# A gated delta rule and a cosine feed-forward block on one core: another order of all work, and pair 1's inverses stored by whole partitions

## The chip, the core and the metric

The kernel runs on one core of a Trainium2 chip. Its five engines take their instructions in the order in which the program lists them, each from its own queue: TensorE (PE, matmuls; PEld is its loading of weights), VectorE (DVE), ScalarE (ACT), GpSimd (POOL) and SyncE (SP). In this program SP does nothing but issue DMAs, and ACT issues some DMAs between its own instructions. An instruction that has to wait holds everything behind it on its engine. The metric is the device time of one execution in microseconds (us), as the median over several runs.

## The reference

Two blocks follow each other. The first is a delta rule over 768 tokens for 4 batches and 8 heads of 48 features. The second multiplies its output, 3072 tokens by 384, by a matrix of 384 by 2048, gates with the cosine, and multiplies by 2048 by 384.

```python
B, H, S, D = q.shape                      # 4, 8, 768, 48
k_n = k / (np.linalg.norm(k, axis=-1, keepdims=True) + 1e-06)
state = np.zeros((B, H, D, D), dtype=np.float32)
for t in range(S):
    kt, vt, bt = (k_n[:, :, t], v[:, :, t], beta[:, :, t, None])
    y[:, :, t] = np.einsum('bhd,bhde->bhe', q[:, :, t], state)
    v_old = np.einsum('bhde,bhd->bhe', state, kt)
    state = state + bt[:, :, :, None] * np.einsum('bhd,bhe->bhde', kt, vt - v_old)
x = y.transpose(0, 2, 1, 3).reshape(B * S, H * D)
h = x @ w_in
g = h * np.cos(h)
out = g @ w_out
```

q, k, v and beta are float32. The two weight matrices arrive as 64-bit floats.

## The kernel before

**The delta rule** is cut into 24 units n of 32 tokens (C). A unit holds all 4 batches and 8 heads. Two units make a pair m. The steps of a unit, with the names that the order uses:

- loads of k, q and v: four DMAs each in the first pairs (`load`, L393 to L411; a load of k for a unit from 6 on takes eight). From unit 6 on, `blocks` (four DMAs for keys, four for queries, L421) bring what the PE transposes (`turn`, L677) brought before.
- `square`, `sum`, `norms`, `scale`: the norms of the keys, on ACT, DVE, POOL and DVE. `weigh` scales a pair's v on DVE.
- `turn` and `turn_out`, then `gram` (L704, 64 recorded matmuls): the products of keys with keys and with queries; `gram_keys` and `gram_queries` on DVE.
- the inverse of a triangular 32 by 32 matrix for every batch and head. Units 0 and 1 build it by `double`, six levels of matmuls on PE, each with a turn, a copy or an addition on DVE or ACT before the next (L788 to L819). Every later pair is inverted by columns on POOL (`invert`, L898, whose two lines are L908 and L915), and goes through DRAM to change its layout: `gram_put` stores the products (g to g_dr, L859), `gram_get` loads them with one matrix to a partition (g_dr to gb, two DMAs, L872 or L880), `invert` runs over the columns in seven blocks `inv.m.0` to `inv.m.6`, `put` stores the result (z to z_dr, one DMA, L920) and `get` loads it for PE (z_dr to zt, four DMAs a unit, L939). Pair 1 (HALVED) is inverted in halves of 16 by 16, in four blocks; its `get` takes eight DMAs a unit (L931), which land in w_sum's space. There is one buffer for gb and one for z, so a pair's inverse starts after the one before it has ended.
- `state` (L959), `right` (L976), `solve` (p_u), `solve_out`, `part_out`, `update` (L1075), `update_out`: the chain from one state to the next. For units 2 and 3 two more products, `solve_half` (p_w, L989) and `between` (p_v), stand before `solve`.
- `within` (L1092), `within_out` and `within_half` (copies to y, L1105 and L1119), `features` (a transpose, p_z, L1127), `features_out`: a unit's output as columns for the second block.

**The second block** takes a pair p of units (256 tokens) at a time. Pair 0 is computed plainly: 32 steps `hidden` (L1148, six recorded matmuls each), the gate in four steps (`turns` on ACT, `rest` on DVE, `cos` on ACT, `gate` on DVE), and 32 steps `out` (L1345, two recorded matmuls each). Pairs 1 to 11 use sums that save products: `x_sum` (L1237) and `left` (L1419) are sums of the inputs and of the gates, on POOL or DVE; `layer` (L1322, eight recorded matmuls) is one of 20 first products, and two parts `out` (L1403, eight each) make one of seven second products. `collect` adds them up, `store` writes.

**The weights** come in 28 chunks (`weights`, one DMA each, L550), and each is turned into float32 by `split` (ACT, L560 and L564), `shift` (DVE, L568) and `add` (POOL, L572).

**Warming**: `keep_warm` (L501) multiplies a tile of ones on PE (L503, two recorded matmuls each), and emits nothing once the first `out` has been emitted. Five of them open the program (WARM_FIRST), and the order holds WARMS more.

**The order of the work** comes from a search and stands in the file: `Order.run` (L227) goes through LINE, a list of 2290 numbers, each a task; it emits them in that order, which is then the order on every engine and on the two DMA queues. OTHER (L63) names the tasks that go to a second engine: DMAs to ACT's queue instead of SP's (`queue`, L387), and with `either` (L390) x_sum to DVE instead of POOL, left to POOL instead of DVE, and inv.1.x to DVE instead of POOL. The end of the file pins every engine to this order.

Of the kernel before, what the change touches and what calls it, by code (L numbers as in the profile page):

```python
# [10 lines left out]
FP = mybir.dt.float32  # L11
# [5 lines left out]
C = 32  # L17
DP = 64
SPLIT = 2
# [41 lines left out]
class Order:  # L61

    OTHER = {  # L63
        ('double_eye', 0), ('v', 2), ('gram_put', 2), ('within_half', 2), ('inv', 1, 0),
        ('put', 1), ('within_half', 3), ('q', 4), ('gram_put', 4), ('gram_get', 2),
        ('blocks', 8, 0), ('k', 9), ('gram_get', 4), ('get', 9), ('gram_put', 10),
        ('gram_get', 5), ('k', 12), ('gram_put', 12), ('v', 13), ('v', 14), ('v', 15),
        ('blocks', 16, 0), ('put', 8), ('blocks', 18, 0), ('get', 19), ('v', 20),
        ('blocks', 20, 1), ('gram_put', 20), ('v', 21), ('gram_get', 10), ('put', 10),
        ('v', 22), ('v', 23), ('put', 11), ('get', 23), ('store', 0, 0), ('right', 2, 2),  # L70
        ('in_sums', 4), ('x_sum', 1, 'd'), ('x_sum', 1, 'n'), ('x_sum', 1, 'm'),
        ('x_sum', 1, 'e'), ('x_sum', 1, 'k'), ('x_sum', 1, 'g'), ('x_sum', 1, 'i'),
        ('x_sum', 1, 'f'), ('x_sum', 1, 'b0'), ('left', 1, 1, 0), ('x_sum', 2, 'd'),
        ('x_sum', 2, 'n'), ('x_sum', 2, 'm'), ('x_sum', 2, 'e'), ('x_sum', 2, 'k'),
        ('x_sum', 2, 'g'), ('x_sum', 2, 'i'), ('x_sum', 2, 'l'), ('x_sum', 2, 'b0'),
        ('left', 2, 4, 0), ('x_sum', 3, 'd'), ('x_sum', 3, 'l'), ('x_sum', 3, 'f'),
        ('x_sum', 3, 'h'), ('x_sum', 3, 'b0'), ('left', 3, 4, 1), ('store', 3, 0),
        ('store', 3, 1), ('x_sum', 4, 'i'), ('x_sum', 4, 'f'), ('x_sum', 4, 'h'),
        ('left', 4, 4, 0), ('left', 4, 4, 1), ('left', 4, 3, 0), ('left', 4, 3, 1),
        ('x_sum', 5, 'd'), ('x_sum', 5, 'm'), ('x_sum', 5, 'e'), ('x_sum', 5, 'k'),  # L80
        ('x_sum', 5, 'g'), ('x_sum', 5, 'f'), ('x_sum', 5, 'b0'), ('left', 5, 1, 0),
        ('left', 5, 2, 0), ('left', 5, 1, 1), ('left', 5, 2, 1), ('left', 5, 4, 0),
        ('left', 5, 3, 0), ('store', 5, 0), ('x_sum', 6, 'd'), ('x_sum', 6, 'n'),
        ('x_sum', 6, 'm'), ('x_sum', 6, 'k'), ('x_sum', 6, 'i'), ('x_sum', 6, 'f'),
        ('x_sum', 6, 'h'), ('x_sum', 6, 'b0'), ('left', 6, 1, 1), ('left', 6, 2, 1),
        ('store', 6, 0), ('store', 6, 1), ('x_sum', 7, 'n'), ('x_sum', 7, 'e'),
        ('x_sum', 7, 'i'), ('x_sum', 7, 'h'), ('x_sum', 7, 'b0'), ('left', 7, 2, 1),
        ('left', 7, 4, 0), ('left', 7, 4, 1), ('left', 7, 3, 1), ('store', 7, 0),
        ('store', 7, 1), ('x_sum', 8, 'n'), ('x_sum', 8, 'e'), ('x_sum', 8, 'k'),
        ('x_sum', 8, 'g'), ('x_sum', 8, 'f'), ('x_sum', 8, 'h'), ('x_sum', 8, 'b0'),  # L90
        ('left', 8, 2, 0), ('left', 8, 3, 1), ('store', 8, 1), ('x_sum', 9, 'd'),
        ('x_sum', 9, 'm'), ('x_sum', 9, 'i'), ('x_sum', 9, 'f'), ('x_sum', 9, 'h'),
        ('x_sum', 9, 'b0'), ('left', 9, 1, 0), ('left', 9, 2, 1), ('left', 9, 4, 1),
        ('store', 9, 0), ('x_sum', 10, 'd'), ('x_sum', 10, 'k'), ('x_sum', 10, 'l'),
        ('x_sum', 10, 'f'), ('x_sum', 10, 'h'), ('left', 10, 1, 0), ('left', 10, 2, 0),
        ('left', 10, 3, 0), ('left', 10, 3, 1), ('x_sum', 11, 'k'), ('x_sum', 11, 'i'),
        ('x_sum', 11, 'f'), ('x_sum', 11, 'h'), ('x_sum', 11, 'b0'), ('left', 11, 1, 0),
        ('left', 11, 4, 1), ('store', 11, 1), ('store_right', 11), ('weights', 5),
        ('weights', 7), ('weights', 12), ('weights', 13), ('weights', 14), ('weights', 15),
        ('weights', 19)  # L100
    }

    WARM_FIRST, WARMS = 5, 20
    LINE = """
# [143 lines left out]
def kernel(  # L248
# [34 lines left out]
    B, H, S, D = q.shape  # L283
# [8 lines left out]
    ROWS = C // SPLIT  # L292
# [66 lines left out]
    DOUBLED, HALVED, HC = 2, 1, C // 2  # L359
# [27 lines left out]
    def queue(*key):  # L387
        return nc.scalar if key in Order.OTHER else nc.sync
# [1646 lines left out]
```

## Time and profile before

| | us |
|---|---|
| median of three runs | 633.37 |
| lowest and highest of them | 633.14, 634.39 |
| the profiled execution, as the other runs are timed | 635.52 |
| its span in the trace | 633.7 |

The profiled execution lasts 1.82 us longer than its span, for what lies before the first and after the last instruction. Section 1 of the page has each engine's busy time; section 2 cuts the span in 40 slices of 15.84 us and gives tenths of busy time. A row of the timeline has the start, the length, the engine, the line and the tiles; "[2.06 <-ACT krec L655]" is idle time of the engine just before, and who ended it. "SPq" and "ACTq" rows are instructions of the sequencer, here DMAs that it issues. In rows by line, the last numbers are the busy time, the mean length of one in ns, and the idle time before them.

### The profile page before, as it was taken

How to read it: one execution, taken by the hardware profiler on the slowest of the kernel's cores; microseconds unless marked ns; L12 is line 12 of the kernel's file. 1: busy time of each engine (PE TensorE's matmuls, PEld its weight loads, DVE VectorE, ACT ScalarE, POOL GpSimd, SP SyncE). 2: the span in 40 equal slices, each digit the busy share in tenths (PEclk: the TensorE clock that was granted, in tenths of full speed). 3: DMA queues.
4: the chain of work that ended last, by engine and by line, in shares of the span. 5: the costliest groups of instructions: out<-in, count | busy, mean ns of one | idle time of the engine just before them, and what ended most of it. 6: DMA issues, size and time to landing. Idle time of an engine off the chain costs nothing.

```text
span 633.7 us, 24406 instructions
## 1 busy us (share of the span) xinstructions
PE 611.1 (96%) x10296; PEld 565.9 (89%) x10296; DVE 481.1 (76%) x969; ACT 326.8 (52%) x610; POOL 430.6 (68%) x784
## 2 busy tenths in 40 slices
PE   7887899999999999999999999999999999999997
PEld 6666787887889999999999999999999999999997
DVE  6876768899998888789868778778758567576582
ACT  3545675563662733745635655555544544455340
POOL 5465888888988887885988898875864884120110
PEclk9998999999999999999999999999999999999999
DMA  8986657744553455346435344234312102100001
GB/s 189 224 189 161 142 117 163 147 74 69 99 88 66 85 88 94 64 68 108 68 65 90 60 78 74 46 57 83 59 32 52 33 13 40 23 2 26 1 26 26
DMA packets 215893, 50.51 MB, mean 80 GB/s; under 512 B 207512, under 2 KB 210856, under 8 KB 215784
## 3 DMA queue, kind: packets, MB, share of 16 engines
q1 hardware_dynamic: 172784, 36.18, 31.4%
q10 hardware_dynamic: 42792, 12.53, 9.6%
q8 instruction: 81, 1.33, 0.9%
q0 software_dynamic: 208, 0.25, 0.2%
q14 instruction: 28, 0.23, 0.1%
HBM read 38.68 MB, written 10.22 MB: 77 GB/s over the span
## 4 chain that ended last, share of the span: by engine, by line
PE 69%; DMA 13%; POOL 8%; DVE 3%; issue 2%; ACT 2%; SPq 2%; ACTq 1%; POOLq 0%; DVEq 0%
PE p_out L1403 27%; PE p_h L1322 25%; DMA kp<-in_k_dram 3%; POOL part L908 3%; PE p_kq L959 3%; POOL z L915 3%; PE p_s L1075 2%; DMA qp<-in_q_dram 2%; PE p_kq L1092 2%; PE p_g L715 2%; PE p_out L1345 2%; DMA w_sum<-in_moe_w_out_dram 2%; PE p_h L1403 2%; DMA w_out<-in_moe_w_in_dram 2%; PE p_u L1033 1%
## 5 line engine op out<-in xcount | busy, mean ns | idle before, releaser
L908 POOL TENSOR_TENSOR part<-z,gb 128x126 f32<-128x126 f32 (+23 forms) x321 | 139.9, 436 | 50.1 <-DMA gb<-g_dr 20.7
L915 POOL TENSOR_TENSOR z<-z,part 128x126 f32<-128x126 f32 (+23 forms) x321 | 146.9, 458 | 25.2
L1403 PE MATMUL p_out<-w_out,g_ffn 128*128 128x192 f32 x672 | 121.7, 329 | 0.3 <-DVE g_ffn L1419 0.3
L1403 PEld LDWEIGHTS p_out<-w_out,g_ffn 128*128 128x128 f32 x672 | 107.8, 190 | 1.9 <-DVE g_ffn L1419 0.5
L1201 ACT ACTIVATE turns<-turns,halfpi 128x512 f32<-128x512 f32 x96 | 68.1, 719 | 74.4 <-DVE turns L1192 61.8
L1322 PE MATMUL p_h<-x_sum,w_in 128*128 128x128 f32 x704 | 93.7, 279 | 0.0
L1403 PE MATMUL p_out<-w_sum,g_ffn 128*128 128x192 f32 x496 | 88.8, 328 | 0.2
L1322 PEld LDWEIGHTS p_h<-x_sum,w_in 128*128 128x128 f32 x704 | 86.3, 191 | 2.9 <-ACT p_h L1334 0.2
L1403 PEld LDWEIGHTS p_out<-w_sum,g_ffn 128*128 128x128 f32 x496 | 79.6, 190 | 1.3 <-POOL g_ffn L1419 0.3
L1339 DVE TENSOR_TENSOR g_ffn<-g_ffn,p_h 128x512 f32<-128x512 f32 x88 | 59.7, 680 | 26.7 <-PE p_h L1322 26.2
L1185 ACT ACTIVATE turns<-g_ffn,quarter_turn 128x512 int32<-128x512 f32 x77 | 54.7, 719 | 45.8 <-DVE g_ffn L1204 19.1
L1204 DVE TENSOR_TENSOR g_ffn<-turns,g_ffn 128x512 f32<-128x512 f32 x77 | 55.5, 726 | 18.3 <-ACT turns L1201 18.1
L1192 DVE SCALAR_TENSOR_TENSOR turns<-g_ffn,turns 128x512 f32<-128x512 f32 x77 | 56.8, 747 | 10.5 <-ACT turns L1185 10.4
L1322 PE MATMUL p_h<-x_sum,in_sum 128*128 128x128 f32 x440 | 58.7, 278 | 0.7 <-ACT p_h L1334 0.7
L1322 PEld LDWEIGHTS p_h<-x_sum,in_sum 128*128 128x128 f32 x440 | 54.4, 191 | 2.6 <-ACT p_h L1334 1.0
L1105 ACT COPY y<-p_kq 32x384 f32<-32x384 f32 x88 | 41.3, 469 | 12.4 <-DMA vp<-in_v_dram 7.1
L1419 POOL TENSOR_TENSOR g_ffn<-g_ffn,g_ffn 128x512 f32<-128x512 f32 x14 | 17.9, 1278 | 43.7 <-PE p_out L1403 27.2
L1322 PE MATMUL p_h<-x_ffn,w_in 128*128 128x128 f32 x352 | 46.7, 277 | 0.0
L606 POOL TENSOR_TENSOR knrm<-ksum,halves 128x16 f32<-128x16 f32 (+1 forms) x14 | 36.8, 2625 | 12.5 <-DVE ksum L594 12.5
L1334 ACT COPY p_h<-p_h 128x512 f32<-128x512 f32 x44 | 25.3, 575 | 37.9 <-PE p_h L1322 23.6
L1322 PEld LDWEIGHTS p_h<-x_ffn,w_in 128*128 128x128 f32 x352 | 42.8, 192 | 1.0
L1455 DVE SCALAR_TENSOR_TENSOR o<-p_out,o 128x192 f32<-128x192 f32 x74 | 25.0, 351 | 23.0 <-PE p_out L1403 21.0
(174 smaller groups left out, 1056.8 us busy)
## 6 DMA issues: line engine op xcount, KB each, us to landing
w_sum<-in_moe_w_out_dram SPq DMA_DIRECT2D x11, 384.0 KB
vp<-in_v_dram SPq DMA_DIRECT2D x64, 48.0 KB
kp<-in_k_dram SPq DMA_DIRECT2D x128, 24.0 KB
gb<-g_dr SPq DMA_DIRECT2D x12, 256.0 KB
w_out<-in_moe_w_in_dram SPq DMA_DIRECT2D x5, 512.0 KB
g_ffn<-in_moe_w_in_dram SPq DMA_DIRECT2D x5, 512.0 KB
out_dram<-o SPq DMA_DIRECT2D x12, 192.0 KB
qp<-in_q_dram SPq DMA_DIRECT2D x34, 64.0 KB
```

What stands on the lines that cost most here:

```text
L606: nc.gpsimd.tensor_tensor(out=scales[m][2][:, part], in0=sums[m, part.start][:, 0:n], in1=halves[:, 0:n], op=ALU.pow,)
L908: eng.tensor_tensor(out=part, in0=z[:, 0:rows, j, None].to_broadcast(shape), in1=a[:, j, None, j + 1 :].to_broadcast(shape), op=ALU.mult,)
L915: eng.tensor_tensor(out=behind, in0=behind, in1=part, op=ALU.subtract)
L1105: nc.scalar.copy(by_parity(y[quarter(b)]), p_kq[quarter(b ^ 1), :, b % 2])
L1185: nc.scalar.activation(turns[p, f], hidden_of(p, f), AF.Identity, bias=quarter_turn, scale=TURN)
L1192: nc.vector.scalar_tensor_tensor(out=r, in0=hidden_of(p, f), scalar=TURN, in1=t, op0=ALU.mult, op1=ALU.subtract,)
L1201: nc.scalar.activation(r, r, AF.Sin, bias=halfpi, scale=2.0 * math.pi)
L1204: nc.vector.tensor_tensor(out=place(p, f), in0=step_of(rests.pop((p, f)), f), in1=step_of(hidden_of(p, f), f), op=ALU.mult,)
L1322: nc.tensor.matmul(p_h[:, e], in_block(*w)[:, e], x_of(p, b), start=new and e == 0, stop=True, skip_group_check=True,)
L1334: nc.scalar.copy(to, part_of(p, one))
L1339: nc.vector.tensor_tensor(out=part_of(p, to), in0=part_of(p, one), in1=part_of(p, two), op=op)
L1403: nc.tensor.matmul(p_o, left(p, part, a)[:, e % 4], right(e, b), start=(e == 0), stop=(e == FT // 2 - 1), skip_group_check=True,)
```

## The change

It has three parts.

1. `put(1)` writes another layout. Before, z_dr of pair 1 is [row, share, unit, head, batch, 16], so that a partition's 16 by 16 matrix is spread over 16 pieces of 64 bytes; now it is [share, unit, head, batch, row, 16], and a partition is one piece of 1 KB. `get` of units 2 and 3 reads the same values from it, still in pieces of 64 bytes. All other pairs are as before.

```diff
     def put(m):
-        width = HC if m == HALVED else C
-        z_drs[m] = dram.tile([ROWS, SPLIT, 2, H, B, width], FP, name="z_dr")
+        if m == HALVED:
+            z_drs[m] = dram.tile([SPLIT, 2, H, B, HC, HC], FP, name="z_dr")
+            queue("put", m).dma_start(
+                out=z_drs[m].rearrange("s u h b r i -> (s u h b) (r i)"),
+                in_=zs.pop(m).rearrange("p r i -> p (r i)"),
+            )
+            return
+        z_drs[m] = dram.tile([ROWS, SPLIT, 2, H, B, C], FP, name="z_dr")
...
-                        in_=z_drs[n // 2][:, a, n % 2, :, b],
+                        in_=z_drs[n // 2][a, n % 2, :, b].rearrange("h r i -> r h i"),
```

2. LINE is another list of all tasks, and WARMS is 22 instead of 20. The tasks that compute the result are the same. 12 warming products stand before the first transpose instead of 7; 23 are emitted in all instead of 24, since the order has its last four behind the first `out`.

3. OTHER is another set. 38 DMA tasks go to ACT's queue instead of 50; 78 x_sums stand on POOL instead of 52, 36 lefts instead of 30, and all double_eye and double_far (4 instead of 1). Of inv.1, blocks 1 and 2 are on DVE instead of block 0.

```diff
     OTHER = {
-        ('double_eye', 0), ('v', 2), ('gram_put', 2), ('within_half', 2), ('inv', 1, 0),
-        ('put', 1), ('within_half', 3), ('q', 4), ('gram_put', 4), ('gram_get', 2),
-        ('blocks', 8, 0), ('k', 9), ('gram_get', 4), ('get', 9), ('gram_put', 10),
...
+        ('double_eye', 0), ('double_far', 0), ('within_half', 0), ('double_eye', 1),
+        ('double_far', 1), ('gram_put', 3), ('inv', 1, 1), ('inv', 1, 2), ('within_half', 3),
+        ('gram_put', 5), ('gram_get', 2), ('put', 2), ('blocks', 9, 0), ('gram_put', 9),
...
-    WARM_FIRST, WARMS = 5, 20
+    WARM_FIRST, WARMS = 5, 22
     LINE = """
-0 1 2 3 9 2178 31 10 4 32 147 33 2182 2186 35 11 36 37 12 5 89 90 91 34 94 95 179 38 29 92 96 13 40
...
+2180 9 10 11 12 13 14 15 0 1 2 5 37 33 34 31 3 91 16 149 38 39 2184 2181 4 92 96 150 35 36 40 97 42
...
```

The DMA tasks in their order, up to the load for unit 4 (`*` is ACT's queue, all others SP's; w is weights, gp gram_put, gg gram_get, b blocks):

```
before: w0 k2 w1 w2 k3 w3 q2 w4 v0 *w5 q3 w6 eye *w7 k4 v1 w8 k5 *gp2 gp3 w9 *q4 w10 gg1 w11
        *v2 *w12 k6 *w13 *w14 q5 *w15 *gp4 k7 w16 *put1 w17 v3 gp5 get2 *gg2 w18 get3 b6.0 *w19
        w20 w21 k8 b6.1 b7.0 b7.1 *k9 v4 w22 w23 w24 w25 v5 gp6 gp7 *b8.0 put2 gg3 w26 get4
after:  w0 k2 w1 q2 w2 v0 w3 k3 w4 q3 w5 k4 w6 v1 w7 gp2 k5 *gp3 w8 q4 *w9 w10 gg1 *w11 eye v2
        w12 w13 w14 k6 q5 *w15 w16 put1 k7 w17 gp4 v3 *gp5 get2 *gg2 *w18 get3 w19 b6.0 v4 w20
        b6.1 b7.0 w21 b7.1 k8 w22 *w23 w24 v5 k9 w25 *put2 gp6 w26 gp7 *w27 get4 gg3
```

On PE, the tasks before solve_half of unit 2 are the same in both but for three: 16 steps `hidden` instead of 15, three steps `out` of pair 0 instead of none, and features of unit 1 behind it instead of before it. Before solve of unit 6 stand one `layer` and one half of a second product less than before.

On POOL, between the first block of pair 2's inverse and the last of pair 6's:

| | add | x_sum | left | right | norms |
|---|---|---|---|---|---|
| before | 11 | 18 | 2 | 1 | 4 |
| after | 10 | 15 | 7 | 0 | 4 |

Up to solve of unit 0, the old order takes the doublings of units 0 and 1 by turns, and the last levels of unit 1 stand behind it; in the new one levels 2 to 5 of unit 1 all stand behind solve of unit 0.

More of the change, by code (lines that the diff above doesn't have):

```diff
@@ L70 @@
[L70 to L99, printed above, removed]
@@ L100 @@
-        ('weights', 19)
+        ('double_eye', 0), ('double_far', 0), ('within_half', 0), ('double_eye', 1),
+        ('double_far', 1), ('gram_put', 3), ('inv', 1, 1), ('inv', 1, 2), ('within_half', 3),
+        ('gram_put', 5), ('gram_get', 2), ('put', 2), ('blocks', 9, 0), ('gram_put', 9),
+        ('put', 4), ('get', 10), ('blocks', 11, 1), ('gram_put', 11), ('v', 12),
+        ('gram_put', 12), ('gram_put', 13), ('gram_get', 6), ('put', 6), ('v', 14),
+        ('gram_get', 7), ('gram_put', 17), ('gram_put', 21), ('gram_put', 22),
@@ new lines @@
+        ('x_sum', 3, 'n'), ('x_sum', 3, 'm'), ('x_sum', 3, 'i'), ('x_sum', 3, 'l'),
+        ('x_sum', 3, 'f'), ('x_sum', 3, 'h'), ('x_sum', 3, 'b0'), ('left', 3, 1, 0),
+        ('left', 3, 4, 0), ('store', 3, 1), ('x_sum', 4, 'n'), ('x_sum', 4, 'g'),
+        ('x_sum', 4, 'l'), ('x_sum', 4, 'f'), ('x_sum', 4, 'h'), ('x_sum', 4, 'b0'),
+        ('left', 4, 1, 0), ('left', 4, 2, 1), ('left', 4, 4, 1), ('left', 4, 3, 0),
+        ('left', 4, 3, 1), ('store', 4, 1), ('x_sum', 5, 'n'), ('x_sum', 5, 'h'),
@@ new lines @@
+        ('left', 5, 3, 0), ('store', 5, 0), ('left', 6, 2, 1), ('left', 6, 4, 0),
+        ('left', 6, 4, 1), ('left', 6, 3, 1), ('store', 6, 0), ('store', 6, 1),
+        ('x_sum', 7, 'm'), ('x_sum', 7, 'e'), ('x_sum', 7, 'l'), ('x_sum', 7, 'h'),
+        ('left', 7, 2, 1), ('left', 7, 4, 0), ('left', 7, 3, 1), ('store', 7, 1),
+        ('x_sum', 8, 'm'), ('x_sum', 8, 'f'), ('x_sum', 8, 'h'), ('left', 8, 1, 0),
+        ('left', 8, 1, 1), ('left', 8, 3, 1), ('store', 8, 0), ('x_sum', 9, 'n'),
@@ new lines @@
+        ('x_sum', 9, 'h'), ('x_sum', 9, 'b0'), ('left', 9, 2, 0), ('left', 9, 1, 1),
+        ('left', 9, 2, 1), ('left', 9, 4, 1), ('left', 9, 3, 0), ('left', 9, 3, 1),
+        ('x_sum', 10, 'd'), ('x_sum', 10, 'h'), ('left', 10, 1, 0), ('left', 10, 2, 0),
+        ('left', 10, 2, 1), ('left', 10, 3, 1), ('store', 10, 0), ('left', 11, 2, 0),
+        ('left', 11, 1, 1), ('store', 11, 1), ('store_right', 11), ('weights', 9),
+        ('weights', 11), ('weights', 15), ('weights', 18), ('weights', 23), ('weights', 27)
```

9 lines of the change are left out of this document (6 added, 3 removed), and 208 rows, old and new, of the table LINE.

## The prediction

> **What bounds the kernel now.** I read the page's busy times first, then the same by stages, since the stages have different limits.
>
> ```profile
> span 633.7 us, 24406 instructions
> PE 611.1 (96%) x10296; PEld 565.9 (89%) x10296; DVE 481.1 (76%) x969; ACT 326.8 (52%) x610; POOL 430.6 (68%) x784
> POOL 5465888888988887885988898875864884120110
> ```
>
> ```profile
> core 0: us, PE busy (x) PEld busy (x) DVE busy (x) ACT busy (x) POOL busy (x), PEclk, DMA share, GB/s
> 0.00:41.00 41.00, 34.06 (x644) 27.74 (x644) 31.21 (x90) 21.30 (x43) 20.13 (x25) 1.00 0.89 198
> 41.00:79.00 38.00, 30.93 (x769) 26.14 (x768) 25.87 (x61) 20.82 (x41) 28.35 (x39) 0.96 0.69 164
> 79.00:125.00 46.00, 44.37 (x1070) 37.21 (x1074) 36.51 (x74) 28.93 (x58) 39.99 (x79) 1.00 0.69 141
> 125.00:286.00 161.00, 158.39 (x2950) 143.71 (x2938) 139.31 (x266) 85.58 (x163) 137.27 (x268) 1.00 0.49 81
> 286.00:634.00 348.00, 343.38 (x4885) 331.08 (x4883) 248.18 (x481) 170.15 (x306) 204.89 (x375) 1.00 0.27 48
> ```
>
> From 79 us on PE is the bound: it idles 1.6 us to 125, 2.6 to 286 and 4.6 after that. Its products are the same in both orders, so time is won only where PE idles or warms: 6.9 us before 41 and 7.1 from 41 to 79.
>
> POOL is the second bound, which its busy share hides:
>
> ```profile
> L915 POOL TENSOR_TENSOR z<-z,part 128x56 f32<-128x56 f32 (+22 forms) x155 | 71.4, 461 | 12.1
> L908 POOL TENSOR_TENSOR part<-z,gb 128x56 f32<-128x56 f32 (+22 forms) x155 | 66.7, 430 | 13.8 <-DMA gb<-g_dr 1.8 <-issue 0.7
> L1419 POOL TENSOR_TENSOR g_ffn<-g_ffn 128x512 f32<-128x512 f32 x3 | 3.8, 1272 | 0.0
> L1237 POOL TENSOR_TENSOR x_sum<-x_sum,x_ffn 128x128 f32<-128x128 f32 x8 | 4.8, 604 | 0.6 <-DVE x_sum L1237 0.3
> L572 POOL TENSOR_TENSOR w_out<-w_out,w_sum 128x384 uint32<-128x384 uint32 x10 | 11.8, 1195 | 0.4 <-issue 0.4
> ```
>
> These are POOL's groups from 79 to 286 us. 155 columns are five inverses (pairs 2 to 6), and with the small gaps between their operations they fill 71.4 + 12.1 + 66.7 + 13.8 = 164.0 of the 207 us, 32.8 each. The other groups take nearly all of the rest. So each inverse starts where POOL's queue lets it, and PE takes the result almost at once: pair 3's last subtraction starts at 160.17, its solve at 169.73.
>
> ```profile
> 160.17 0.23 POOL L915 TENSOR_TENSOR z<-z,part 128x16 f32<-128x16 f32 x1
> 169.73 0.68 PE L1033 MATMUL p_u<-rhs,zt 64*64 64x48 f32 x32
> ```
>
> From an inverse's end to its solve are thus about 9.3 us (store, load, landing).
>
> **The start: ACT's queue.** Which wait keeps PE idle around 46 to 51?
>
> ```profile
> 39.12 2.98 ACTq L408 DMA_DIRECT2D qp<-in_q_dram  x4
> 45.91 3.08 ACTq L408 DMA_DIRECT2D vp<-in_v_dram  x4
> 49.03 0.47 ACT L1105 COPY y<-p_kq 32x384 f32<-32x384 f32 x1 [4.95 <-DMA vp<-in_v_dram]
> 51.29 0.52 PE L1127 MATMUL p_z<-consts,y 128*128 128x128 f32 x3 [2.06 <-ACT krec L655]
> ```
>
> ACT issues v of unit 2 and cannot copy y meanwhile; y's transpose comes at 51.29, and state, hidden steps and DVE's first block of pair 1's inverse stand behind it. The change puts both loads on SP and the first block on POOL. Up to 4.95 us go from that wait; what is late next is SP.
>
> **SP's queue.** To be followed are pair 1's inverse and the two loads that release the rest:
>
> ```profile
> 39.99 2.10 SPq L872 DMA_DIRECT2D gb<-g_dr x2
> 46.88 6.68 SPq L408 DMA_DIRECT2D kp<-in_k_dram  x8
> 53.66 3.02 SPq L408 DMA_DIRECT2D qp<-in_q_dram  x4
> 56.73 5.58 SPq L408 DMA_DIRECT2D kp<-in_k_dram  x8
> 63.42 1.91 SPq L408 DMA_DIRECT2D vp<-in_v_dram  x4
> 69.88 0.39 SPq L859 DMA_DIRECT2D g_dr<-g  x1
> 70.38 5.50 SPq L931 DMA_DIRECT2D w_sum<-z_dr  x8
> ```
>
> ```profile
> 51.18 0.17 DVE L908 TENSOR_TENSOR part<-z,gb 128x15 f32<-128x15 f32 x1
> 61.44 0.23 POOL L915 TENSOR_TENSOR z<-z,part 128x15 f32<-128x15 f32 x1
> 61.70 0.38 ACTq L920 DMA_DIRECT2D z_dr<-z  x1
> 78.68 1.43 PE L989 MATMUL p_w<-rhs,w_sum 32*32 32x48 f32 x64
> ```
>
> - Pair 1's gram_get: four loads of q (2.98) are now ahead of it on SP, one chunk of weights (0.4) is not: 39.99 + 2.6 = 42.6, issued by 44.7. Its inverse took 61.67 − 51.18 = 10.5; it now starts between 44.7 (loaded at once) and 51.2 (as before). I take 48, since landings here need some 3 us; it ends at 58.5.
> - SP reaches put(1) after v (3.1), k (6.7), q (3.0) and five single DMAs (2.0): 59.5. So SP, not the inverse, is last. Then put (0.4), k (5.6), two singles (0.8), v (1.9): get of unit 2 at 68.2, where it was 70.38. Before, SP had stood from 65.33 to 69.88 for unit 5's gram_put, which now waits on ACT; behind it there are cos of the first hidden steps, which have POOL's additions as cover. The gain is 2.2. Bounds: +5.0 if SP issues at 0.48 a DMA (the row of v: 1.91 for 4), so that the inverse's end at 58.5 is the limit; −3.0 if nothing on SP moves up and the 6.1 us of both loads and two more singles come on top of 65.33.
> - p_w followed 8.3 us after that issue: 76.5 instead of 78.68.
>
> The put in whole partitions: landing of a put is shown for pair 2.
>
> ```profile
> 110.42 4.12 DMA g_dr<-g
> 114.60 3.87 DMA z_dr<-z
> ```
>
> From put(1) to get on SP there were 8.7 us and will be 8.3, so 3.87 are covered with 4.4 to spare; I cost this edit at nothing. Without that cover it could give back at most 3.87, and could lose only what the get would pay for other addresses; its pieces stay 64 bytes, so I take 0 there too.
>
> **What PE does before p_w.** One hidden step and three output steps more, one transpose less.
>
> ```profile
> 75.24 3.51 PE L1148 MATMUL p_h<-x_ffn,w_in 128*128 128x128 f32 x30
> 106.42 1.46 PE L1345 MATMUL p_out<-w_out,g_ffn 128*128 128x384 f32 x4
> ```
>
> That is 3.51/5 + 3 × 1.46/2 − 0.5 = 2.4 us of work, moved into the 7.1 us of idle time. At p_w PE is then 2.2 + 2.4 = 4.6 us ahead.
>
> Five more warming products ahead of the first transpose hold it back by about 3 us, at most:
>
> ```profile
> 1.36 5.76 PE L503 MATMUL p_out<-o 128*128 128x256 f32 x14 [1.36 <-DVE o L323]
> ```
>
> (5.76/7 each cold; those after it are shorter.) They cost nothing if the first doubling waits for the norms, which now stand behind beta on DVE; without that cover the doublings are 3 us later, and y with them. I take 0, since y's gain of up to 4.95 above is larger than what I used. The one warming product less is in the idle time already.
>
> **How much POOL lets through.**
>
> ```profile
> 73.04 1.19 ACTq L880 DMA_DIRECT2D gb<-g_dr  x2
> 78.97 0.32 POOL L908 TENSOR_TENSOR part<-z,gb 128x31 f32<-128x31 f32 x1 [0.33 <-DMA gb<-g_dr]
> ```
>
> Pair 2's inverse starts 5.9 us after its gram_get. That needs unit 4's gram_put landed: SP at 68.2 − 2.3 = 65.9, plus 4.1: 70.0. So inverse 2 starts at 76.0, 3.0 us earlier. To inverse 3's end POOL has one addition of weights less (1.2): 4.2 us earlier, at 156.2, and solve of unit 6 can run at 165.5. PE, 4.6 ahead and with a layer and half a product less before it (about 2.2), would want it at 162.9. It waits 2.6, and 2.0 of the gain is left. To inverse 6 POOL has five lefts more and one add, three x_sums and a right less: 5 × 1.27 − 1.2 − 3 × 0.6 − 1.0 = 2.4 us; POOL's own waits there can take that up, and before its lag at unit 12 was larger than 9.3.
>
> Later, DVE loses 26 x_sums and ACT twelve DMA tasks; PE's idle time there is 2.6 + 4.6, of which the last few us are the end's. I take 0.9 back, bounds −3 (new waits as large as the old) to +3.
>
> **Sum.** 2.0 + 0.9 = 2.9 off the profiled span of 633.7: 630.8. That execution took 1.8 more than its span and 2.15 more than the median of the runs; against the median, 633.4 − 2.9 = **630.5**.
>
> **Rivals.**
>
> - *POOL lets all through.* The order has the inverse earlier than I reckon (loads land sooner, bound +5.0). Then PE keeps 4.6 and gets 0.9 + 0.3 of its other waits: 627.6. For it: SP's rows contain waits for landings, which may shrink. Against: POOL has no free time to 286.
> - *Slower: POOL's longer queue.* Place: POOL between inverses 2 and 6. If gram_get for pair 2 on ACT leaves no earlier than 73.04 (the turns and unit 5's gram_put are ahead of it), inverse 2 starts at 78.97 and the 2.4 us come in full, 635.8. It decides from a start of 76.6 on, 78.97 − 2.4. For it: every us of POOL before 286 is taken. Against: its gaps, some 5 us there.
> - *No change that counts.* The early us only make PE wait at solve of unit 6 and for units 8 and 10, so that the gain is hidden behind the same inverses: 633.4.
> - *The clock.* PE's clock fell once:
>
> ```profile
> 56.00:60.00 4.00, 3.71 (x52) 3.21 (x52) 3.03 (x10) 2.68 (x6) 3.22 (x11) 0.70 0.63 134
> 60.00:64.00 4.00, 4.00 (x113) 3.59 (x112) 1.69 (x4) 1.89 (x5) 3.43 (x8) 0.87 0.79 129
> ```
>
> That cost (1 − 0.70) × 4 + (1 − 0.87) × 4 = 1.7 us, after idle stretches of which the longest is the 2.06 above. In the new order an output step stands before p_w, so no warming product is left to fill a wait there; if PE idles at p_w as long as it did at 51, the clock falls there and 1.7 come on top: 632.2.
> The Trainium skill ("TensorE: Matmul & The Clock Gate", "What's actually happening") says that a monitor of PE's activity halves the clock after an idle window of about 3.4 us. By that rule a wait of 2 us would be harmless; the dip behind 2.06 us says that a window which is idle in part is enough.
>
> **Chances.** Forecast 0.40 (its own range 629 to 632.5), POOL lets all through 0.26, slower 0.18, no change 0.10, clock 0.06. The range goes to both other cases and their bounds, 624.5 to 636. What a measurement of this kernel can tell from no change is about 0.2%, 1.3 us: faster 0.64 (0.40 × 0.9 + 0.26 + a third of 0.06), slower 0.19, the same 0.17.
>
> **What would show it.** ACT has no 4.95 us before the first copy of y, and y's transpose stands before 47. get of unit 2 is issued at 68 and p_w at 76 to 77; the put lands well before. POOL's inverse of pair 2 starts at 76, that of pair 3 ends at 156, and PE waits for zt at unit 6. If p_w is not earlier than 78, SP's queue took all; if inverse 3 ends after 158, the slower case holds; if it ends before 154 without a wait on PE, the gain is nearer 6 us.

## The result, and the profile after

| | us |
|---|---|
| the kernel before, median | 635.04 (6 runs) |
| the changed kernel, median | 637.93 (6 runs, 636.84 to 639.38) |
| ratio | 1.0049, 95% interval 1.0026 to 1.0072 |
| the changed kernel's profiled execution; its span | 636.84; 635.1 |

The change costs about 2.9 us where a gain of 2.9 was forecast; the time lies above the range. Five executions of the experiments below, of 642 to 2069 us, ran in a slow state and are left out of all figures, one of them the profiled one of the old layout in the new order. The page of the changed kernel, with its busy times:

```profile
span 635.1 us, 24407 instructions
PE 611.8 (96%) x10294; PEld 567.6 (89%) x10294; DVE 475.8 (75%) x944; ACT 327.3 (52%) x610; POOL 454.2 (72%) x809
```

By stages, at the same limits as before (the columns are busy times, PEclk the granted clock):

```profile
0.00:41.00 41.00, 34.23 (x674) 28.10 (x674) 30.79 (x86) 21.80 (x44) 22.95 (x28) 0.96 0.89 199
41.00:79.00 38.00, 33.34 (x805) 28.30 (x805) 32.25 (x75) 21.90 (x44) 27.06 (x35) 0.96 0.64 163
79.00:125.00 46.00, 40.45 (x935) 33.76 (x935) 30.27 (x64) 27.57 (x56) 37.08 (x71) 0.93 0.71 145
125.00:286.00 161.00, 159.00 (x2999) 144.85 (x2989) 138.74 (x270) 86.62 (x164) 139.97 (x267) 1.00 0.47 77
286.00:634.00 348.00, 344.77 (x4907) 332.59 (x4892) 243.75 (x451) 169.42 (x304) 227.17 (x412) 1.00 0.27 49
286.00:635.10 349.10, 344.77 (x4907) 332.59 (x4892) 243.75 (x451) 169.42 (x304) 227.17 (x412) 1.00 0.27 49
```

PE's idle time fell by 2.4 us from 41 to 79 (7.07 to 4.66). After 125 it hardly fell: each kernel taken to the end of its own span (633.7 and 635.1, hence the last row), it is 6.3 us where it was 6.9. From 79 to 125 it rose from 1.63 to 5.55, and the clock there, 1.00 before, is 0.93. The clock was also low once before 41. These 46 us lose more than all other stages win.

The early milestones came as forecast. The transpose of y, on PE:

```profile
46.66 0.90 PE L1126 MATMUL p_z<-consts,y 128*128 128x128 f32 x3
```

SP's queue, from put of pair 1 to its get (two units in one row):

```profile
58.87 0.56 SPq L913 DMA_DIRECT2D z_dr<-z  x1
59.47 4.82 SPq L401 DMA_DIRECT2D kp<-in_k_dram  x8
64.39 0.38 SPq L543 DMA_DIRECT2D w_sum<-in_moe_w_out_dram  x1
64.87 0.39 SPq L852 DMA_DIRECT2D g_dr<-g  x1
65.31 2.19 SPq L401 DMA_DIRECT2D vp<-in_v_dram  x4
67.54 13.36 SPq L930 DMA_DIRECT2D w_sum<-z_dr  x16
```

And PE's rows that waited, from p_w of unit 2 on:

```profile
77.76 0.86 PE L988 MATMUL p_w<-rhs,w_sum 32*32 32x48 f32 x58 [0.61 <-DMA w_sum<-z_dr]
79.24 0.55 PE L1126 MATMUL p_z<-consts,y 128*128 128x128 f32 x3 [0.62 <-ACT g_ffn L1000]
80.36 0.88 PE L988 MATMUL p_v<-g_ffn,in_sum 32*32 32x48 f32 x64 [0.57 <-ACT x_ffn L1134]
...
93.14 0.44 PE L988 MATMUL p_w<-rhs,w_sum 32*32 32x48 f32 x20 [0.98 <-issue]
94.16 0.88 PE L988 MATMUL p_v<-g_ffn,in_sum 32*32 32x48 f32 x64 [0.57 <-ACT g_ffn L1000]
99.98 0.88 PE L1091 MATMUL p_kq<-u_all,tt 32*32 32x48 f32 x64 [0.69 <-DVE u_all L1052]
118.19 4.50 PE L1321 MATMUL p_h<-x_sum,w_in 128*128 128x128 f32 x24 [2.20 <-ACT p_h L1333]
```

p_w's first products ran at 76.9, but 58 of the 64 only from 77.8, when get's last pieces had landed. Behind it stands only the transpose of unit 1 (`features`, 79.24). It is written to the same bank of PSUM as p_w and p_v (`bank("two", ...)`, which has one buffer), so PE waits twice: 0.62 us until ACT has copied p_w, and 0.57 until ACT has copied the transpose. For unit 3 nothing at all stands between p_w and p_v. The same place in the kernel before, PE's timeline:

```profile
74.91 0.49 PE L1127 MATMUL p_z<-consts,y 128*128 128x128 f32 x3
...
78.68 1.43 PE L989 MATMUL p_w<-rhs,w_sum 32*32 32x48 f32 x64
80.04 0.94 PE L1148 MATMUL p_h<-x_ffn,w_in 128*128 128x128 f32 x6
80.91 0.88 PE L989 MATMUL p_v<-g_ffn,in_sum 32*32 32x48 f32 x64
81.72 2.27 PE L1148 MATMUL p_h<-x_ffn,w_in 128*128 128x128 f32 x18
```

Here the transpose came ahead of p_w, and a hidden step (80.04) covers the copy. So p_v came only 0.55 us earlier in the new order (80.36 against 80.91), and its waits go on at unit 3. The longest, 2.20 us at 118, starts on SP's queue and ACT:

```profile
102.87 3.81 SPq L401 DMA_DIRECT2D vp<-in_v_dram  x4
106.72 4.79 SPq L401 DMA_DIRECT2D kp<-in_k_dram  x8
```

```profile
114.58 0.84 ACT L582 ACTIVATE g_ffn<-kp 128x768 f32<-128x768 f32 x1 [3.44 <-DMA kp<-in_k_dram]
```

k of unit 9, which ACT's queue had issued at 97.91 before, now stands behind v on SP. ACT waits 3.44 us for it with the squares, and the copies out of PSUM that PE needs stand behind them. This wait is not in every execution: with k of unit 9 in the same place, ACT does not wait for it in the profiles of two kernels below (warming at p_w, three steps back). What such a wait does to PE's clock, by stretches of 3.4 us:

```profile
92.00:95.40 3.40, 1.85 (x101) 1.51 (x89) 0.68 (x2) 1.07 (x2) 2.85 (x8) 1.00 0.57 87
95.40:98.80 3.40, 3.40 (x50) 3.18 (x52) 1.23 (x4) 2.38 (x5) 3.24 (x5) 0.50 0.72 144
116.00:119.30 3.30, 1.11 (x10) 1.11 (x11) 3.30 (x7) 2.95 (x7) 2.14 (x3) 1.00 0.88 172
119.30:122.70 3.40, 3.40 (x18) 3.40 (x17) 3.40 (x6) 1.66 (x4) 3.40 (x2) 0.50 0.97 257
```

PE is busy for 1.85 of 3.4 us, and in the next 3.4 us, when it has full work, its clock is 0.50; the same again at 119. Each such fall can cost up to half of its 3.41 us, 1.7 us.

### The profile page after: what moved, and what is told of

Same layout as the page of the kernel before. It is cut to its first block, busy times and chain, and to the rows that moved or that the text cites. A ratio compares the mean times of both kernels' runs of the same rounds, so it can differ in the third digit from the quotient of the medians.

```text
span 635.1 us, 24407 instructions
## 1 busy us (share of the span) xinstructions
PE 611.8 (96%) x10294; PEld 567.6 (89%) x10294; DVE 475.8 (75%) x944; ACT 327.3 (52%) x610; POOL 454.2 (72%) x809
## 4 chain that ended last, share of the span: by engine, by line
PE 52%; POOL 26%; DMA 11%; issue 4%; SPq 4%; DVE 2%; ACTq 1%; ACT 0%; POOLq 0%; DVEq 0%
PE p_out L1402 23%; PE p_h L1321 20%; POOL part L901 11%; POOL z L908 10%; DMA kp<-in_k_dram 3%; SPq L401 3%; DMA g_dr<-g 2%; PE p_kq L958 2%; DMA vp<-in_v_dram 2%; POOL knrm L599 2%; PE p_h L1402 2%; DMA gb<-g_dr 1%; PE p_s L1074 1%; PE p_kq L1091 1%; POOL g_ffn L1418 1%
## 5 line engine op out<-in xcount | busy, mean ns | idle before, releaser
L901 POOL TENSOR_TENSOR part<-z,gb 128x126 f32<-128x126 f32 (+24 forms) x317 | 141.0, 445 | 33.8 <-DMA gb<-g_dr 4.8
L908 POOL TENSOR_TENSOR z<-z,part 128x126 f32<-128x126 f32 (+24 forms) x317 | 145.1, 458 | 24.8
L1203 DVE TENSOR_TENSOR g_ffn<-turns,g_ffn 128x512 f32<-128x512 f32 x77 | 59.8, 782 | 19.7 <-ACT turns L1200 19.7
L1418 POOL TENSOR_TENSOR g_ffn<-g_ffn,g_ffn 128x512 f32<-128x512 f32 x20 | 26.4, 1324 | 62.2 <-PE p_out L1402 51.5
```

The lines of the kernel that those rows point to most:

```text
L901: eng.tensor_tensor(out=part, in0=z[:, 0:rows, j, None].to_broadcast(shape), in1=a[:, j, None, j + 1 :].to_broadcast(shape), op=ALU.mult,)
L908: eng.tensor_tensor(out=behind, in0=behind, in1=part, op=ALU.subtract)
L1203: nc.vector.tensor_tensor(out=place(p, f), in0=step_of(rests.pop((p, f)), f), in1=step_of(hidden_of(p, f), f), op=ALU.mult,)
L1418: either(("left", p, x, s), nc.vector, nc.gpsimd).tensor_tensor(out=left(p, s, to), in0=left(p, s, one), in1=left(p, s, two), op=op)
```

## The experiments

Times scatter by some 2 us between executions of one kernel, so each kernel of this section was run up to 12 times (one of the mixes 8 times) beside the kernel before. The changed kernel itself was not run again beside them; its 1.0049 comes from its own six runs. One profile is one draw. The line numbers differ from kernel to kernel, since the list fills other lines.

**First: the layout, and k of unit 9.** The old layout in the new order (the diff of part 1 undone):

> The changed kernel with one part undone: pair 1's inverses are stored in the old layout [row, share, unit, head, batch, 16] again. Theory L (the layout is the loss): the sixteen loads of get for units 2 and 3 took 13.36 us of SP's queue in the changed kernel and 11.6 before (5.50 + 5.73 + 0.4 between them), and SP never waits for anything else from 81 to 112 us, so everything on SP comes 1.7 us earlier without the new layout: k of unit 9 lands at 112.7 instead of 114.4, products p_w of unit 2 at 75 instead of 76.9, and the time falls by 1.5 to 3 us against the changed kernel. Theory K (k of unit 9 behind v of unit 5 on SP is the loss): within 0.5 us of the changed kernel, and ACT still waits 3 us for kp before the squares at 114.

k of unit 9 earlier (SP's order):

```diff
-  k8 w22 w24 v5 k9 w25
+  k8 k9 w22 w24 v5 w25
```

> The changed kernel with k of unit 9 (eight DMAs on SP) issued ahead of chunk 22 of the weights, so ahead of chunk 24 and of v of unit 5, instead of behind them. Theory K: the load is issued some 5 us earlier and lands at about 109.5; ACT's wait of 3.44 us before the squares goes, PE's wait of 2.20 us at 118 goes, and with it the clock's fall at 119.3 (1.7 us): 2.2 to 3.9 us off the changed kernel, about 634.5 where it takes 637.9. Theory L: at most 0.5 us.

Both edits:

> The changed kernel with both edits: old layout and k of unit 9 ahead of chunk 22. If the two causes are separate, the gains add up. If the layout's only effect is that it delays k of unit 9 on SP, this equals the kernel with the early k alone, within 0.5 us.

And the new layout alone, in the kernel before:

> The kernel before with only the new layout of pair 1's z_dr; its order and queues untouched. The prediction's step (the edit costs nothing): within 0.6 us of the kernel before, since put has 8 us until the first get. Theory L: the sixteen gets take some 1.7 us more of SP's queue, p_w of unit 2 starts at 80 instead of 78.7, and the kernel is 1.5 us slower.

| kernel | ratio to the kernel before | interval |
|---|---|---|
| old layout, new order | 1.0048 | 1.0020 to 1.0077 |
| k of unit 9 early | 1.0065 | 1.0040 to 1.0090 |
| both | 1.0070 | 1.0039 to 1.0100 |
| new layout, old order | 0.9998 | 0.9973 to 1.0023 |

The layout is not the loss, from either side: theory L fell. Theory K fell too. With k early ACT did not wait for it, but for something else. ACT's and PE's rows of that kernel:

```profile
104.79 0.36 ACTq L496 DMA_DIRECT2D w_sum<-in_moe_w_out_dram  x1
105.25 0.95 ACT L1069 COPY y<-p_kq 32x384 f32<-32x384 f32 x2 [7.06 <-POOL part L854]
```

```profile
107.21 0.91 PE L1079 MATMUL p_z<-consts,y 128*128 128x128 f32 x3 [5.50 <-ACT y L1057]
```

ACT stood 7.06 us at a single DMA that it issues, y's copies behind it came late, and PE waited 5.50. The releaser named is not the true one: the trace's semaphore records show that this DMA shares its semaphore with one of k's, issued by SP at 102.86, whose sixteen parts landed from 104.35 to 104.71; ACT issued its DMA at 104.79. A wait was exchanged for a larger one.

**Second: mixes of both orders.** Each takes the tasks of one order up to a point and all others in the other order, with their queues and engines; all four have the new layout.

> The first part of the new order (332 tasks, up to the product p_v of unit 2 at 80 us, with their queues and engines), and behind it all other tasks in the order and on the engines of the kernel before. Theory S (the time was lost between 79 and 125 us, by the order of that stretch): PE's time above the short task lengths fell by 2.6 us before 79, rose by 5.8 from 79 to 125 and fell by 1.4 after that, and these add up, so this kernel is 1.5 to 2.6 us faster than the kernel before. Rival P (POOL's inverses hold PE, as the prediction's sum had it): what is won early is waited for at solve of unit 6, so no difference above 0.7 us. Rival C (each execution gets its own falls of the clock, and the order only shifts them): within 1 us of the kernel before, with as many falls as the changed kernel has.

> The reverse: the order of the kernel before up to p_v of unit 2, then the rest in the new order. Theory S: the early 2.6 us are not won and the 5.8 are lost: 3 to 4.4 us slower than the kernel before, so the slowest of the four. Rival P: as slow as the changed kernel, 2 to 3 us. Rival C: between the two kernels.

> The new order up to solve of unit 4 (124 to 128 us), then the rest as in the kernel before. Theory S: the loss is already inside, and the new order's 1.4 us after 125 are not won: 3 us slower than the kernel before. Rival P: if the loss were made by POOL's longer queue between inverses 2 and 6, it would be mostly gone here: within 1 us of the kernel before.

> The order of the kernel before up to solve of unit 4, then the new one. Theory S: the loss is not inside: 0 to 1.4 us faster than the kernel before. Rival P: POOL's longer queue up to 286 us is inside: 2 to 3 us slower than the kernel before.

| begins with | up to | goes on with | ratio | interval |
|---|---|---|---|---|
| new | p_v of unit 2 | old | 1.0012 | 0.9982 to 1.0041 |
| old | p_v of unit 2 | new | 1.0088 | 1.0056 to 1.0119 |
| new | solve of unit 4 | old | 1.0016 | 0.9991 to 1.0042 |
| old | solve of unit 4 | new | 1.0088 | 1.0061 to 1.0116 |

No theory had all four. The new beginning with the old rest is neither slower nor faster beyond doubt, and a gain of 1.5 to 2.6 us, as theory S had it, is not there; the old beginning with the new rest came out slower than the whole new order, though their intervals overlap. PE's rows of the first of these two say that a mix makes waits of its own:

```profile
84.71 2.93 PE L1293 MATMUL p_out<-w_out,g_ffn 128*128 128x384 f32 x4 [5.39 <-POOL w_out L514]
```

The new order's output steps expect weights that POOL had added earlier in its own beginning. The mixes therefore show how tightly both parts fit each other, and can't place the loss.

**PE's account over the profiles of these kernels.** From PE's timeline, for each of its tasks, I took the time from its start to the start of the next, less the tenth percentile of its kind: what idle time and low clock add. In sums, us:

```
                                       to p_v of    p_v of unit 2 to    after it
                                       unit 2       solve of unit 4
the kernel before                      27.4          5.3                22.1
  new layout                           25.9          5.9                22.0
  old beginning to solve of unit 4     26.4          5.7                29.7
the changed kernel                     25.3         11.1                20.1
  k of unit 9 early                    25.8         11.5                21.1
  k early and old layout               29.4          8.8                22.4
  new beginning to solve of unit 4     26.6          7.1                22.1
```

Between executions the first column scatters more than the orders differ. The middle one does not: 5.3 to 5.9 with the old order, 7.1 to 11.5 with the new. In these profiles the loss lies between p_v of unit 2 and solve of unit 4, and ahead of it no gain is clear of the scatter. The order of that stretch alone does not make it: the mix that changes to the old order at p_v of unit 2, taken the same way, has 9.8 in the middle, with the clock at half from 78.6 to 85.4, behind a wait at p_w.

**Third: the clock, the squares, and the loads at the start.** Warming products at p_w of unit 2 (they are added work, into columns nobody reads):

```diff
         if not out_begun:
             nc.tensor.matmul(p_out[:, 0], out_tiles[0][:, 0:128], out_tiles[0][:, 128:DM])
+        elif len(out_begun) < 16:
+            for _ in range(4):
+                nc.tensor.matmul(
+                    p_out[:, 1, 128:HM], out_tiles[0][:, 0:128], out_tiles[0][:, 128:HM],
+                    start=False, stop=False,
+                )
...
-  out.0.0.2 solve_half.2
+  out.0.0.2 warm.18 warm.19 warm.20 warm.21 solve_half.2
```

> The changed kernel with warming products just ahead of p_w of unit 2: the four warm tasks that come to nothing behind the first output step now emit four products of 64 columns each there (sixteen, an estimate of 1.7 us from 0.43 us for 256 columns), into columns of the output's bank that nobody reads. Four of the five profiles with the new order up to there show PE waiting 1.6 to 4.8 us at p_w, and three of them the clock at half behind it for 6.8 us. Theory C (the clock makes a wait dear): the wait hides the products, the clock no longer falls at 78 to 85, mean clock up by 0.002 to 0.003, time down by 1 to 2 us against the changed kernel. Theory D (the wait alone costs, the clock falls while PE has little to do): no gain, or up to 0.5 us more.

The squares later (ACT's order; the sum on DVE goes behind update_out.3):

```diff
-  put.2 square.4 cos.0.14 layer_out.1.1 split.25 layer_out.1.5 w27
+  put.2 cos.0.14 layer_out.1.1 split.25 layer_out.1.5 square.4 w27
```

> The changed kernel with the squares of units 8 and 9 on ACT moved behind two copies out of PSUM (layer_out of products 1 and 5, 120 tasks of the list at most apart), and their sum on DVE behind the update of the state, so that nothing that PE needs stands behind the wait for k of unit 9. Theory A (waits of ACT and DVE for a late load are what PE loses from 82 to 125): PE's wait of 2.20 us at 118 cannot come back; 1 to 3 us faster than the changed kernel. Theory Q (SP's full queue is late anyway, and another load becomes the one that is waited for): within 0.7 us.

Both:

> Both edits. With theories C and A the gains add to 2 to 4 us, and the kernel is about as fast as the kernel before; with D and Q it stays 2 to 3 us slower.

And in the kernel before:

```diff
-        ('double_eye', 0), ('v', 2), ('gram_put', 2), ('within_half', 2), ('inv', 1, 0),
-        ('put', 1), ('within_half', 3), ('q', 4), ('gram_put', 4), ('gram_get', 2),
+        ('double_eye', 0), ('gram_put', 2), ('within_half', 2), ('inv', 1, 0),
+        ('put', 1), ('within_half', 3), ('gram_put', 4), ('gram_get', 2),
```

> The kernel before with one edit: q of unit 4 and v of unit 2 (four DMAs each) are issued on SP, at their places in the list, and not on ACT. By the prediction's step (ACT's wait of 4.95 us holds PE at 51 us and the removal is a gain): the transpose of y starts before 48 instead of 51.3, and the kernel is 0 to 3 us faster. Rival G (p_w of unit 2 waits for get of unit 2 on SP whatever PE does before it): the transpose comes as early, but eight more DMAs of some 0.5 us stand on SP ahead of get, p_w is done 2 to 4 us later than before, and the kernel is 1.5 to 4 us slower.

| kernel | ratio | interval | mean clock of its runs |
|---|---|---|---|
| the changed kernel | 1.0049 | 1.0026 to 1.0072 | 0.9910 |
| warming at p_w | 1.0025 | 1.0002 to 1.0047 | 0.9953 |
| squares later | 1.0036 | 1.0013 to 1.0060 | 0.9918 |
| both | 1.0057 | 1.0032 to 1.0083 | 0.9934 |
| old order, two loads on SP | 0.9978 | 0.9947 to 1.0008 | 0.9955 |

The kernel before had a mean clock of 0.9958 in its 156 runs beside the experiments. With the products at p_w the clock is nearly all back, as theory C said, but with the later squares beside them only half of it (0.9934). On the time theory C is only half supported: the ratio halves, but the intervals touch, and with the squares later beside it nothing of that is left. The squares alone fit neither theory well: 0.8 us better, inside the scatter. Rival G fell: p_w of unit 2 came at 80.1, 1.4 us later than before where G said 2 to 4, and the kernel is not slower. The transpose of y came at 49.26 in that profile, not before 48 as both theories had it.

**Fourth: the covers.** Three output steps back between the products of units 2 and 3 (PE's order):

```diff
-  out.0.0.0 hidden.0.6.1 hidden.0.6.2 hidden.0.6.3 out.0.0.1 out.0.0.2
-  solve_half.2 features.1 between.2
+  hidden.0.6.1 hidden.0.6.2 hidden.0.6.3
+  solve_half.2 features.1 out.0.0.0 between.2
...
-  solve_half.3 between.3
+  solve_half.3 out.0.0.1 between.3
...
-  solve.3 within.3
+  solve.3 out.0.0.2 within.3
```

> The changed kernel with three output steps of pair 0 moved on PE from ahead of p_w of unit 2 to behind it: one between p_w and p_v of unit 2, one between p_w and p_v of unit 3, one between solve and within of unit 3. Theory F: PE reaches p_w 2.2 us earlier and waits that much longer for its loads, but the idle 0.57, 0.57 and 0.68 us go and with them the clock's fall behind unit 3 (1.7 us): 1 to 3 us faster than the changed kernel. Theory Q: the longer wait at p_w is not made up, within 0.7 us of the changed kernel or up to 1.5 slower, since the clock falls at p_w every time.

With warm.18 to warm.21 ahead of solve_half.2:

> The same with the four warm tasks that came to nothing ahead of p_w of unit 2 (0.43 us each, which the longer wait there hides). Theory F with the clock: 1 us faster still than with the three steps alone, mean clock 0.995 or more. If idle time alone counts: no difference from the three steps alone.

The reverse in the kernel before:

```diff
-  solve_half.2 hidden.0.6.3 between.2
+  hidden.0.6.3 solve_half.2 between.2
...
-  solve_half.3 hidden.0.12.0 hidden.0.12.1 between.3
+  hidden.0.12.0 hidden.0.12.1 solve_half.3 between.3
```

> The kernel before with three hidden steps moved ahead on PE: the one between p_w and p_v of unit 2 to ahead of that p_w, and the two between p_w and p_v of unit 3 to ahead of that p_w. Nothing else moves. Theory F: PE idles some 0.57 us at each p_v that it did not before, and part of the executions get a fall of the clock behind it: 1 to 2.5 us slower than the kernel before. Theory Q: no load is touched, within 0.7 us.

The three steps and the later squares together:

> The changed kernel with the three output steps behind p_w of unit 2 and with the squares of units 8 and 9 behind two copies out of PSUM. Theory F+A (covers and the wait for k of unit 9 together): 2.5 to 4 us faster than the changed kernel, within 0.7 us of the kernel before. Theory Q (some other late load takes their place): 1.3 to 2 us slower than the kernel before, as with the three steps alone.

| kernel | ratio | interval | mean clock |
|---|---|---|---|
| three steps back | 1.0035 | 1.0011 to 1.0059 | 0.9912 |
| and warming at p_w | 1.0027 | 1.0001 to 1.0053 | 0.9929 |
| three steps back and squares later | 1.0019 | 0.9989 to 1.0049 | 0.9924 |
| the kernel before, covers away | 1.0007 | 0.9986 to 1.0029 | 0.9947 |

With the steps back, from 79 to 125 us:

```profile
79.00:125.00 46.00, 44.77 (x1016) 36.41 (x1017) 32.36 (x71) 27.71 (x56) 38.53 (x75) 0.93 0.69 144
```

PE idles 1.23 us there, not 5.55: the place is repaired. But the work that was put back had stood in the wait at p_w. PE's rows of the same kernel:

```profile
76.36 0.27 PE L941 MATMUL p_w<-rhs,w_sum 32*32 32x48 f32 x4
78.03 0.27 PE L941 MATMUL p_w<-rhs,w_sum 32*32 32x48 f32 x2 [1.40 <-DMA w_sum<-z_dr]
79.31 1.34 PE L941 MATMUL p_w<-rhs,w_sum 32*32 32x48 f32 x58 [1.01 <-DMA w_sum<-z_dr]
81.27 0.90 PE L1079 MATMUL p_z<-consts,y 128*128 128x128 f32 x3 [0.62 <-ACT g_ffn L953]
```

p_v follows at 83.38, seven us behind p_w's first product: PE idles for 3.0 of them, and from 79.5 on its clock is 0.50. With the warm products beside the steps ACT's wait for k of unit 9 was back (ACT's and PE's timelines):

```profile
112.79 0.84 ACT L535 ACTIVATE g_ffn<-kp 128x768 f32<-128x768 f32 x1 [3.47 <-DMA kp<-in_k_dram]
```

```profile
116.39 1.83 PE L1274 MATMUL p_h<-x_sum,w_in 128*128 128x128 f32 x14 [3.07 <-ACT p_h L1286]
```

Taking the covers from the kernel before made just the idle time that F names. PE's rows of that kernel:

```profile
81.68 0.88 PE L942 MATMUL p_v<-g_ffn,in_sum 32*32 32x48 f32 x64 [0.60 <-ACT g_ffn L954]
...
97.48 0.71 PE L942 MATMUL p_v<-g_ffn,in_sum 32*32 32x48 f32 x48 [0.60 <-ACT g_ffn L954]
```

Yet 1.0007 is less than F's 1 to 2.5 us (1.0016 to 1.0039), though its interval reaches 1.0029, and in the profile the clock did not fall there. So theory F is not borne out in the time: two short gaps alone cost little, if anything that these runs can tell. F+A expected the two edits within 0.7 us of the kernel before: 1.0019 is 1.2 us, with an interval that holds both that and half of the loss.

PE's account, taken over these profiles as above, says where the time went. Between p_v of unit 2 and solve of unit 4 the changed kernel has 11.1 us; warming has 8.1, the later squares 8.5, both 6.5, the three steps back 4.5, these with warming 7.9 and with the later squares 4.3. So the repairs work in their place, in one profile each. But ahead of p_v the three steps back have 4.2 us more than the changed kernel, and with the later squares 4.9 more: the wait at p_w. And behind solve of unit 4 a bound appears that I had overlooked. PE's and POOL's timelines of the kernel with the steps back and the later squares:

```profile
164.37 2.05 PE L1274 MATMUL p_h<-x_sum,w_in 128*128 128x128 f32 x16 [2.63 <-POOL x_sum L1189]
```

```profile
159.27 0.42 POOL L861 TENSOR_TENSOR z<-z,part 128x16 f32<-128x16 f32 x1
159.65 3.34 POOL L552 TENSOR_TENSOR knrm<-ksum,halves 128x16 f32<-128x16 f32 x1
162.96 0.63 POOL L1189 TENSOR_TENSOR x_sum<-x_ffn 128x128 f32<-128x128 f32 x1
163.67 0.65 POOL L1189 TENSOR_TENSOR x_sum<-x_sum,x_sum 128x128 f32<-128x128 f32 x1
```

The second x_sum stands on POOL behind inverse 3 and the norms, and PE waits for it. Of the eleven profiles with the new order from solve of unit 4 on, ten have this wait, 0.8 to 3.1 us long; of the eight with the old order there, none. The one without it is the changed kernel: there PE came so late that it needed this x_sum just as it was ready (163.5). So what a repair wins before 163 us PE mostly waits for here, which fits that the edits don't add up. No run moved this x_sum, and all repairs leave features of unit 1 between p_w and p_v; what either is worth was not tried.

**A version that beats both?** The parts that cost nothing, in the old order:

> The kernel before with the new layout and with q of unit 4 and v of unit 2 on SP. If the 0.22% of the second edit was real: 634.2 where the kernel before takes 635.5. If it was chance: within 0.1% of the kernel before.

It was run a second time:

> The order of the kernel before, with the new layout and q of unit 4 and v of unit 2 on SP, measured a second time. If the gain of 0.2% was real: 0.9975 to 0.9990 of the kernel before. If chance: 0.9995 to 1.001.

0.9980 (0.9955 to 1.0005) and 0.9986 (0.9955 to 1.0018). Each time 0.9 to 1.3 us in the right direction, with an interval that still holds 1; it is faster than the changed kernel, and not shown to be faster than the kernel before.

## Why the prediction was wrong, step by step

- *ACT's queue at the start.* Right in the trace (y's transpose at 46.66, forecast before 47). Too large in the bound: the 4.95 us went, and the same edit alone in the old order brought the transpose to 49.26 and a ratio of 0.9978, which may be nothing.
- *SP and get of unit 2.* Forecast at 68.2, measured 67.54. p_w forecast at 76.5, measured 76.86.
- *The layout costs nothing.* Right in the time, by two experiments. The old layout is not free on SP: in the new order with the old layout (the kernel with both edits) the eight loads behind put took 8.54 us of SP, and with the new layout 4.46 to 5.56 in ten profiles:

```profile
59.54 8.54 SPq L354 DMA_DIRECT2D kp<-in_k_dram  x8
```

  In the old order, with both loads on SP, get of unit 2 was issued at 71.8 with the old layout and at 66.2 and 66.6 with the new, but that is no price of the layout: with the old one SP had stood from 66.4 to 71.3 for unit 5's gram_put, whose products came late on PE.
- *"At p_w PE is then 2.2 + 2.4 = 4.6 us ahead."* This is the step that failed, twice. First, "p_w followed 8.3 us after that issue" priced the first product; the last pieces of get decide, and p_v came 0.55 us earlier, not 2.2. Second, the hidden step among the 2.4 us of work "moved into the 7.1 us of idle time" was the cover of unit 2. I counted features of unit 1 behind p_w as a transpose less, where it is a second wait for ACT on the way to p_v, and did not ask what stood between p_w and p_v afterwards. From p_w of unit 2 to solve of unit 3 PE has ten hidden steps where it had twelve and an output step, and none of them between p_w and p_v. The idle 0.62 and 0.57 us at unit 2, and 0.57 and 0.69 at unit 3, are the answer.
- *"Later … I take 0.9 back, bounds −3 … to +3."* After 125 us PE's idle time fell by 0.6, somewhat less than forecast. But the term left out 79 to 125 altogether, as if nothing could be lost there: twelve DMA tasks leave ACT, and I counted them as relief. k of unit 9 among them went behind v on SP, and ACT's squares waited 3.44 us for it. Idle time in this stage rose by 3.9 us. What is behind a load that moves to another queue has to be asked for each, as I did for unit 5's gram_put and for no other.
- *The rival "slower", and how much POOL lets through.* The rival's sign was right, its place not for the changed kernel. Pair 2's inverse started at 77.65 (forecast 76.0; the rival decides from 76.6 on), and inverse 3 did end after 158 (its last subtraction, on POOL):

```profile
77.65 0.24 POOL L901 TENSOR_TENSOR part<-z,gb 128x31 f32<-128x31 f32 x1 [0.66 <-DMA gb<-g_dr]
158.35 0.56 POOL L908 TENSOR_TENSOR z<-z,part 128x16 f32<-128x16 f32 x1
```

  But that is 1.5 us earlier than in the kernel before, and PE did not wait for it. The 2.6 us that the sum had PE wait at solve of unit 6 are not there. PE's timeline:

```profile
168.61 0.68 PE L1032 MATMUL p_u<-rhs,zt 64*64 64x48 f32 x32
```

  In the changed kernel the time was lost ahead of it, and PE's idle time from 125 to 286 fell from 2.6 to 2.0. That POOL holds PE in this place was right all the same: it shows where PE comes earlier, at the x_sum behind inverse 3 (up to 3.1 us), and not at the solve.
- *The rival "clock"* named a cause that was at work, but neither its places nor what sets it off. I gave one fall, 1.7 us and 0.06; the profile has four, at 16.9, 44.2, 95.4 and 119.3 us, where the kernel before has one. By the mean clock of the runs (0.9910 against 0.9958) the new order loses up to 0.0048 × 634 = 3.0 us to it; the warming products, which bring the clock back, bring back about half of the time. The stretches at half clock last 3.41 us each, and no idle time of that length stood ahead of any: 1.85 us of work in 3.4 was little enough. It is not the single wait of 2 us that I took it for, either: in the kernel before, the 3.41 us from 47.35, with 1.52 us of work and most of the wait of 2.06, were followed by the full clock, and those from 54.18, with 2.04 us of work, by the half. Where the limit lies is open. The Trainium skill ("TensorE: Matmul & The Clock Gate", "What's actually happening") speaks of an idle window of about 3.4 us that is not aligned to the kernel's start; the length agrees, idle throughout it need not be.

Shown is that the layout isn't the cause, and, in the profiles, where the loss lies. That missing covers, a late load and the clock make it is read from the traces and not shown in the time: no repair of the new order is told apart from the changed kernel by its interval, and none is faster than the kernel before. The share of each is open, and so is how much of a repair POOL's x_sum at 163 us lets through.

## What to carry to other kernels

Work that is pulled forward into idle time is work that covered something later; look at what stands between each pair of dependent products after the move before counting the gain. When a DMA changes its queue, follow its first reader and everything behind that reader. A wait on PE is to be priced with the clock that follows it. And before a repair is tried, look which engine would hold the work next.

## What the runs showed of the hardware

- The time of one kernel varies with its clock falls. Of the 156 runs of the kernel before beside the experiments, the 75 with a mean clock of 0.997 or more took 634.5 us on average, the 81 others 636.5; in the five groups of runs the difference is 0.5 to 3.4. So a search that doesn't see the clock can lose by it what it wins in idle time.
- A DMA that ACT issues can hold ACT for 7 us though nothing in its data is late. In the trace's records the DMAs of both queues take eight semaphores in turn, and an issue comes when the DMA before it on its semaphore has landed: in four profiles, of 674 pairs of successive issues on one semaphore, 650 to 652 have all sixteen landings of the first between them. By these records a full SP queue holds ACT, too, and the two queues together issue no faster than eight DMAs in the time that one takes to land.
